# A PSUM bank for each row half of the products with v, five banks shared by both kinds of scores, and one bank for the dense products

## The chip, the core and the metric

The kernel runs on one core of a Trainium2 chip. The metric is the device time of one execution in microseconds (us). The core has a matrix engine (PE in the profile), a vector engine (DVE), a scalar engine (ACT), a general engine (POOL, GpSimd) and a queue for transfers (SP). The PE writes its results to PSUM, which has eight banks of 128 x 512 fp32 values here; DVE and ACT read them from there.

## What is computed

The kernel takes x (2048 x 512) and adds two branches that start from the same normalised rows. The reference, cut to what matters:

```
xn = layernorm(x)
q, k, v = split(xn @ wqkv)                 # 32 heads of 16
o = softmax(q @ k.T * 16 ** -0.5) @ v      # each head, 2048 x 2048 scores
out = x + o @ wo + gelu(xn @ w1 + b1) @ w2 + b2     # w1: 512 x 1792, w2: 1792 x 512
```

The results have the precision of fp32: a dense product is made of three fp16 products (high by high, high by low, low by high; `PAIRS` in the kernel).

## The kernel before

The attention is cut into 32 tiles t (8 groups of 4 heads, 4 blocks of 512 queries), and a tile into 16 units. One call of `unit` (L582) issues one unit of the first pass over the scores and, 20 units behind (`LEAD`), one unit of the second pass.

- First pass, `s_half` (L238): the scores of one head (128 queries by 512 keys) go to a bank with the tag "S", and DVE takes their maximum over the keys (L250). There are four a unit, called S0 to S3 below.
- Second pass, `e_half` (L282): the scores of one head, keys by queries and less the maximum, go to a bank with the tag "T", and ACT writes their exponential to SBUF as `pe` (L295). There are four a unit, E0 to E3.
- Products with v, `v_half` (L298): four heads by 64 rows (keys) in fp32, added up over the 16 units of a tile. There are two halves a unit. Both add to one bank (tag "V"); at the end of a tile ACT copies it to `osb` (L321).
- Dense products: everything else (the projections to q and k of later groups, called P below; the two layers of the feed-forward branch, H for the hidden one and Y for the output; the projection with wo, O) is a list of `Group`s (L408). `dense` (L565) issues three or four products of the current group in each half of a unit (`pace`: FAST, MEAN, SLOW). A P or H group has 12 products for each row half, a Y group 42.

The PE is used as eight tiles of 64 rows by 32 columns, so that an operand of 64 rows needs half of the rows, and two different streams run in the two row halves. `unit` writes the order out by hand. The first half of a unit issues S0 (rows 0 to 63), E1 (rows 64 to 127), S1 (rows 64 to 127), E0 (rows 0 to 63), then products with v in rows 64 to 127 and dense products in rows 0 to 63. The second half issues S2 (0 to 63), E3 (64 to 127), S3 (64 to 127), E2 (0 to 63), then products with v in rows 0 to 63 and dense products in rows 64 to 127. The order on every engine is the order of the program.

Since the bank of the products with v is written from the one row half and then from the other, and the bank of a dense group too, the first product of a half waits until the last products of the half before have ended: `leave` (L176) lets them count a semaphore up, and `enter` (L185) makes the next product wait for it. This is called the turn.

Banks: S has three (0 to 2), T three (3 to 5), D and V one each (L102), but a group or tile that begins takes a fresh bank from the other list and gives its own back when it ends (`hold`, L112; L303, L324, L400, L438). A bank is written again only when its reader is done: S(k+3) waits for the reduction of S(k), and the exponentials' scores for the third exponential before.

What a unit leaves for later (transfers, steps on POOL) is put in slots by `later` (L204), one slot a unit. After the first pass has ended (512 units), 20 more units run the second pass out; then `land` and the end of the program do what dense products are left.

Of the kernel before, what the change touches and what calls it, by code (L numbers as in the profile page):

```python
# [47 lines left out]
def layer_kernel(ctx: ExitStack, tc: tile.TileContext, x, wqkv, wo, w1, b1, w2, b2, out):  # L48
# [16 lines left out]
    w1_d = dram.tile([NF, P, 2, NC, P], F16, name="w1_d")  # L65
# [36 lines left out]
    free_banks = {"S": [0, 1, 2], "T": [3, 4, 5], "D": [6], "V": [7]}  # L102
# [98 lines left out]
    mt_of, ptiles, pv_of = {}, {}, {}  # L201
# [108 lines left out]

    def v_end(u):
# [12 lines left out]
        if t == NG * NQB - 1:  # L324
            later(1, lambda: last_one(osb))
            return
# [7 lines left out]

        def inverse():
            nc.vector.reciprocal(dn, dn)
            given("dve", 330)
            later(1, lambda: nc.sync.dma_start(den_d[t, 1].rearrange("h (c q) -> (h c) q", q=32), dn))
# [5 lines left out]
        def store():  # L344
# [4 lines left out]
                   (0, lambda: later(1 if n == 1 else 6, put)))  # L349
# [8 lines left out]
        n, far = (2, 3) if t < (NG - 1) * NQB else (1, 0)  # L358
        later(1, sums)
        later(2, lambda: nc.sync.dma_start(dn, den_d[t, 0].rearrange("h (c q) -> (h c) q", q=32)))  # L360
        later(2 + n + far, inverse)
        later(3 + 2 * n + far, spread)
        later(4 + 3 * n + far, store)
# [32 lines left out]
    def dbank():  # L396
        turn[0] += 1
        if pos[0] < LEAD:
            return banks("T"), None
        return hold("D", "T")  # L400

    class Group:
# [32 lines left out]
        def end(self):  # L435
            self.finish(self.bank)
            if self.key is not None:
                free_banks["T"].append(self.key)  # L438
# [35 lines left out]
    def project(m, w, sb, wh, bank, early=False):  # L474
# [6 lines left out]
        def finish(pj):  # L481
# [4 lines left out]
            stg = ph.tile([P, 2, QB], F16, name="stg", bufs=2)  # L486
# [4 lines left out]
            else:  # L491
# [5 lines left out]
                else:  # L497
                    hi = lambda: nc.gpsimd.tensor_scalar(stg[:, 0], pf, 1.0, 0.0, op0=ALU.mult, op1=ALU.add)
                    lo = lambda: nc.gpsimd.tensor_tensor(stg[:, 1], pf, stg[:, 0], op=ALU.subtract)
                    later(1, lambda: pooled((620, hi), (1160, lo), (0, lambda: later(3, put, True))), True)  # L500
# [28 lines left out]
    pos, spent, cur = [0], [False], [None]  # L529
    feed, xbs, wcs = [], {}, {}  # L530

    def fetch_x(b):
        if b < NQB:
            xbs[b] = feed[0].tile([P, 2, NC, QB], F16, name="xb", bufs=1)
            nc.sync.dma_start(xbs[b], xn_d[:, :, :, b * QB:(b + 1) * QB])

    def fetch_w1(n):
        if n < NQB * NF:
            wcs[n] = feed[0].tile([P, 2, NC, P], F16, name="wc", bufs=3)
            nc.sync.dma_start(wcs[n], w1_d[n % NF])  # L540
# [24 lines left out]
    def dense(gen, side):  # L565

        f = group(gen)
# [5 lines left out]
    def land():  # L573

        for side in range(2):
# [6 lines left out]
    def unit(gen):  # L582
# [4 lines left out]
        if u == LEAD and cur[0] is not None:  # L587
            burst(gen, cur[0].left())
        pos[0] += 1
        for a in range(2):  # L590
# [5 lines left out]
            if e >= 0:  # L596
# [33 lines left out]
    with ExitStack() as st1:  # L630
# [10 lines left out]
        def chunk(src):  # L641
            wf = ph.tile([P, 4 * W], F32, name="wch", bufs=3)
            v = wf.rearrange("p (a b) -> p a b", b=src.shape[2])
            nc.sync.dma_start(v, src)
# [14 lines left out]
        loads = []  # L659
# [13 lines left out]
        wvv = wqkv[:, 2 * D:3 * D].rearrange("(c p) n -> p c n", p=P)  # L673
        wvf = [chunk(wvv[:, :, i * W:(i + 1) * W]) for i in range(2)]
        wvh = [ph.tile([P, NC, D], F16, name="wvh", tag="wsp", bufs=2) for _ in range(2)]
# [32 lines left out]
        free = ["T", "D", "T", "V", "T", "S", "S"]  # L708
# [102 lines left out]
        free[:] = ["T", "D", "T", "V", "T"]  # L811
# [68 lines left out]
        def prepare():  # L880
# [20 lines left out]
            for n in range(16):  # L901
# [5 lines left out]
                def then(wh=None, n=n):  # L907
                    ended[0] = True
                    later(3, lambda: put(wh, n), True)

                def put(wh, n):
                    if n < 7:
                        for a in range(2):
                            for l in range(2):
                                nc.sync.dma_start(w1_d[2 * n + a][:, l], wh[:, l, :, a * P:(a + 1) * P])
                    elif n < 14:
                        nc.sync.dma_start(w2_d[:, :, 2 * n - 14:2 * n - 12, :], wh)
# [5 lines left out]
                wh = ph.tile([P, 2, 4, W] if n < 7 else [P, 2, 2, D], F16, name="wsp", bufs=2)  # L923
                k = n if n < 7 else 8
                split_steps(wh[:, 0], wh[:, 1], v, inv[:, k:k + 1], lambda wh=wh, then=then: then(wh))
# [12 lines left out]
    def mlp():  # L938
# [25 lines left out]
        for b in range(NQB):  # L964
            xb = xbs[b]
            g = m2.tile([P, 2, NF, QB], F16, name="g", bufs=1)
            for f in range(NF):
                later(1, lambda n=b * NF + f + 2: fetch_w1(n))
                wc = wcs[b * NF + f]
                if b == 0 and f >= 3:  # L970
                    nc.sync.dma_start(w2_s[:, :, f - 3:NF if f == NF - 1 else f - 2, :],
                                      w2_d[:, :, f - 3:NF if f == NF - 1 else f - 2, :])
# [156 lines left out]
```

## Time and profile before

| | |
|---|---|
| time, median of 3 runs | 1569.33 us (1568.03 to 1570.18) |
| the profiled execution | 1564.89 us |
| its span, first to last instruction | 1563.1 us |
| granted PE clock | 0.995 |
| PE, DVE, ACT, POOL busy | 97%, 91%, 88%, 42% of the span |
| reductions L250 | 2048, 683 ns each |
| exponentials L295 | 2048, 687 ns each |

All numbers of the trace come from this one execution. A row of the profile names line, engine, operation, the tiles that it writes and reads, its shape and its count; behind the bar stand the busy time, the mean of one, and the idle time before it with what ended it. PE rows hold matmuls that overlap, so their sum means little; the start times of the streams tell more. One S, E or dense stream is four matmuls side by side (count x4).

### The profile page before, as it was taken

How to read it: one execution, taken by the hardware profiler on the slowest of the kernel's cores; microseconds unless marked ns; L12 is line 12 of the kernel's file. 1: busy time of each engine (PE TensorE's matmuls, PEld its weight loads, DVE VectorE, ACT ScalarE, POOL GpSimd, SP SyncE). 2: the span in 40 equal slices, each digit the busy share in tenths (PEclk: the TensorE clock that was granted, in tenths of full speed). 3: DMA queues.
4: the chain of work that ended last, by engine and by line, in shares of the span. 5: the costliest groups of instructions: out<-in, count | busy, mean ns of one | idle time of the engine just before them, and what ended most of it. 6: DMA issues, size and time to landing. Idle time of an engine off the chain costs nothing.

```text
span 1563.1 us, 85813 instructions
## 1 busy us (share of the span) xinstructions
PE 1513.9 (97%) x38915; PEld 810.6 (52%) x38915; DVE 1424.6 (91%) x2420; ACT 1369.7 (88%) x2254; POOL 654.0 (42%) x678
## 2 busy tenths in 40 slices
PE   8998989999999999999999999999999999999988
PEld 3434545555555555555555555555555555554433
DVE  8899878899999999999999999999999999998801
ACT  4317879999999999999999999999999999998983
POOL 3113667657771113768211277741137772110000
PEclk9999999999999999999999999999999999999999
DMA  6455665532221201131111211131012201002323
GB/s 205 129 154 187 206 159 189 168 96 78 69 62 60 61 27 42 42 81 42 49 28 47 63 42 32 48 89 36 28 49 61 56 22 35 26 21 87 105 72 111
DMA packets 120246, 123.69 MB, mean 79 GB/s; under 512 B 38988, under 2 KB 90572, under 8 KB 119880
## 3 DMA queue, kind: packets, MB, share of 16 engines
q1 hardware_dynamic: 119880, 118.21, 25.8%
q8 instruction: 304, 4.98, 1.4%
q14 instruction: 62, 0.51, 0.1%
HBM read 80.61 MB, written 37.34 MB: 75 GB/s over the span
## 4 chain that ended last, share of the span: by engine, by line
PE 73%; DVE 17%; DMA 4%; issue 3%; SPq 1%; POOL 1%; ACT 1%; DVEq 0%; POOLq 0%; ACTq 0%
PE pV L169 22%; PE pD L169 17%; PE pS L169 15%; PE pT L169 15%; DVE mt L250 12%; DVE hh L979 2%; DMA m_d<-mhl 1%; PE pD L426 1%; PE pT L426 1%; DMA oc<-ot_d 1%; PE pT L519 1%; SPq L392 1%; DVE amx L648 0%; POOL osb L346 0%; PE pV L519 0%
## 5 line engine op out<-in xcount | busy, mean ns | idle before, releaser
L295 ACT ACTIVATE pe<-pT,sexp 128x512 f32<-128x512 f32 x2048 | 1268.2, 687 | 80.8 <-PE pT L169 35.0
L250 DVE TENSOR_REDUCE mt<-pS 128x1 f32<-128x512 f32 x2048 | 1288.3, 683 | 38.4 <-PE pS L169 22.8
L169 PE MATMUL pV<-pe,vv 64*32 64x512 f32 x8192 | 1082.6, 598 | 2.0 <-issue 0.9
L169 PE MATMUL pT<-qst,kst 64*32 64x512 f16 x8192 | 709.9, 379 | 14.0 <-DMA qst<-m_d 8.9
L169 PE MATMUL pS<-kst,qst 62*32 62x512 f16 x8192 | 637.7, 379 | 19.9 <-DVE mt L250 15.9
L169 PEld LDWEIGHTS <-qst 62*32 62x32 f16 x8192 | 279.5, 92 | 253.1 <-issue 115.9
L169 PEld LDWEIGHTS <-kst 64*32 64x32 f16 x8192 | 294.6, 91 | 187.7 <-issue 76.3
L169 PE MATMUL pD<-w_s,g 64*32 64x512 f16 x5376 | 365.4, 377 | 0.4 <-issue 0.4
L169 PE MATMUL pD<-xb,wc 64*32 64x512 f16 x5376 | 360.8, 377 | 0.0
L169 PEld LDWEIGHTS pV<-pe,vv 64*32 64x32 f32 x8192 | 181.9, 105 | 101.6 <-PE pS L169 7.6
L169 PEld LDWEIGHTS <-wc 64*32 64x32 f16 x5376 | 120.1, 91 | 52.7 <-issue 1.9
L997 POOL TENSOR_TENSOR xa<-xa,yt 128x512 f32<-128x512 f32 x16 | 20.5, 1278 | 283.3 <-ACT yt L995 283.3
L169 PEld LDWEIGHTS <-g 64*32 64x32 f16 x5376 | 111.5, 91 | 46.1 <-issue 2.1
L346 POOL TENSOR_TENSOR osb<-osb,rb 128x512 f32<-128x512 f32 x31 | 39.9, 1286 | 223.6 <-DMA rb<-den_d 176.2
L169 PE MATMUL pD<-xt,wqk_h 64*32 64x512 f16 x1920 | 128.6, 380 | 0.6 <-issue 0.6
L959 POOL TENSOR_TENSOR t<-hh 128x512 f32<-128x512 f32 x56 | 58.3, 1041 | 144.4 <-DVE hh L979 130.3
L961 POOL TENSOR_TENSOR t<-t,hh 128x512 f32<-128x512 f32 x56 | 71.8, 1282 | 4.7
L954 POOL TENSOR_TENSOR t<-t,hh 128x512 f32<-128x512 f32 x56 | 71.7, 1280 | 4.7
L956 POOL TENSOR_TENSOR g<-t,g 128x512 f16<-128x512 f32 x56 | 65.3, 1165 | 4.7
L169 PEld LDWEIGHTS <-wqk_h 64*32 64x32 f16 x1920 | 44.1, 92 | 20.3 <-issue 5.1
L169 PE MATMUL pD<-wo_s,oc 64*32 64x512 f16 x768 | 53.0, 392 | 0.4 <-issue 0.2
L979 DVE TENSOR_SCALAR hh<-pD,fac,b_s 128x512 f32<-128x512 f32 x56 | 45.3, 809 | 1.2
(137 smaller groups left out, 817.7 us busy)
## 6 DMA issues: line engine op xcount, KB each, us to landing
wch<-in_B_w_dram SPq DMA_DIRECT2D x28, 512.0 KB
wc<-w_d SPq DMA_DIRECT2D x56, 256.0 KB
qk_d<-stg SPq DMA_DIRECT2D x32, 256.0 KB
rb<-den_d SPq DMA_DIRECT2D x124, 64.0 KB
kst<-qk_d SPq DMA_DIRECT2D x128, 48.0 KB
qst<-qk_d SPq DMA_DIRECT2D x128, 48.0 KB
xs<-in_A_x_dram SPq DMA_DIRECT2D x16, 256.0 KB
qk_d<-stg SPq DMA_DIRECT2D x32, 128.0 KB
```

Of the source, the lines that this page charges most:

```text
L169: p = nc.tensor.matmul(*args, **kw)
L250: nc.vector.reduce_max(mt_of[t][:, n, qt, kb:kb + 1], s, axis=AX.X)
L295: nc.scalar.activation(pe, st, AF.Exp, scale=sexp[:, g // 2:g // 2 + 1])
L346: pooled((1280, lambda: nc.gpsimd.tensor_tensor(osb, osb, rb, op=ALU.mult)), (620, lambda: nc.gpsimd.tensor_scalar(ot[:, 0], osb, 1.0, 0.0 ...
L392: nc.sync.dma_start((qst, kst)[w][g % 2][p][b][64 * a:64 * a + 48, :], qk_d[w, h * DH:(h + 1) * DH, :, b * QB:(b + 1) * QB].rearrange("d j ...
L426: nc.tensor.matmul(self.bank, lhs, rhs, start=start, stop=self.last and self.over())
L954: (1280, lambda: nc.gpsimd.tensor_tensor(t1, t1, hh, op=ALU.mult)),
L956: (1160, lambda: nc.gpsimd.tensor_tensor(g[:, 1, f, :], t1, g[:, 0, f, :], op=ALU.subtract)),
L959: pooled((1040, lambda: nc.gpsimd.tensor_tensor(t1, hh, hh, op=ALU.mult)), (620, lambda: nc.gpsimd.tensor_scalar(t1, t1, 1.0, 1.0 / GELU_A ...
L961: (1280, lambda: nc.gpsimd.tensor_tensor(t1, t1, hh, op=ALU.mult)),
L979: nc.vector.tensor_scalar(hh, hp, scale, bias, op0=ALU.mult, op1=ALU.add)
L997: add = lambda: nc.gpsimd.tensor_tensor(xa, xa, yt, op=ALU.add)
```

## The change

It gives each row half of the products with v a bank of its own (6 and 7) with no turn; the first half's bank is copied by ACT half a unit earlier, and DVE adds the second one to it. From unit 20 on, S and T draw from one list of five banks (0 to 4). A dense group always has bank 5, only the dense products keep the turn, and after a group has ended `dense` leaves out one half of a unit. All H groups run at the FAST pace (before: every second one SLOW), all Y groups at MEAN (before: SLOW in the first two blocks). Transfers are cut smaller and put into slots further apart. The core of the diff:

```diff
-    w1_d = dram.tile([NF, P, 2, NC, P], F16, name="w1_d")
+    w1_d = dram.tile([NF // 2, P, 2, 2, NC, P], F16, name="w1_d")
...
-    free_banks = {"S": [0, 1, 2], "T": [3, 4, 5], "D": [6], "V": [7]}
+    free_banks = {"S": [0, 1, 2], "T": [3, 4], "D": [5], "V": [6, 7]}
...
-        if kt == 0 and a == 0:
-            pv_of[t] = hold("V", "S")
-        pv = pv_of[t][0]
+        if kt == 0:
+            pv_of[t, a] = bank_tile(6 + a, "V")
+        pv = pv_of[t, a]
...
-            product("V", pv[32 * h:32 * h + 32, :], vv[r, kt, c:c + 32], ptiles[u, h][r],
-                    start=(kt == 0 and a == 0), stop=(kt == 15 and a == 1))
+            product(None, pv[32 * h:32 * h + 32, :], vv[r, kt, c:c + 32], ptiles[u, h][r],
+                    start=kt == 0, stop=kt == 15)
+        if kt == 15 and a == 0:
+            osbs[t] = work.tile([P, QB], F32, name="osb", bufs=2)
+            nc.scalar.activation(osbs[t], pv_of.pop((t, 0)), AF.Copy)
+            given("act", 600)
...
-        pv, k = pv_of.pop(t)
-        osb = work.tile([P, QB], F32, name="osb", bufs=2)
-        nc.scalar.activation(osb, pv, AF.Copy)
-        given("act", 600)
-        free_banks["S"].append(k)
+        osb = osbs.pop(t)
+        nc.vector.tensor_tensor(osb, pv_of.pop((t, 1)), osb, op=ALU.add)
+        given("dve", 700)
...
-        n, far = (2, 3) if t < (NG - 1) * NQB else (1, 0)
-        later(1, sums)
...
+        at = (1, 3, 6, 7, 9, 12) if t < (NG - 1) * NQB else (1, 2, 5, 6, 7, 8)
+        for k, fn in zip(at, (sums, turned, inverse, keep, spread, store)):
+            later(k, fn)
...
-        if pos[0] < LEAD:
+        if pos[0] < LEAD or pos[0] >= NU + LEAD:
             return banks("T"), None
-        return hold("D", "T")
+        return hold("D", "D")
...
-            stg = ph.tile([P, 2, QB], F16, name="stg", bufs=2)
+            stg = ph.tile([P, 2, QB], F16, name="stg", bufs=3)
...
-            nc.sync.dma_start(xbs[b], xn_d[:, :, :, b * QB:(b + 1) * QB])
+            for c in range(NC):
+                later(1 + c, lambda c=c: nc.sync.dma_start(xbs[b][:, :, c], xn_d[:, :, c, b * QB:(b + 1) * QB]))
...
             done, cur[0] = cur[0], None
             done.end()
+            pause[0] = True
...
+        if pause[0]:
+            pause[0] = False
+            return
         f = group(gen)
...
-        if u == LEAD and cur[0] is not None:
-            burst(gen, cur[0].left())
+        if u == LEAD:
+            if cur[0] is not None:
+                burst(gen, cur[0].left())
+            free_banks["S"] = free_banks["T"] = free_banks["S"] + free_banks["T"]
...
-                new = r == 0 and w % 16 == 0
-                if live and not new:
+                if live:
                     v_half(w, r)
                 dense(gen, 1 - r)
-                if live and new:
-                    v_half(w, r)
-
-                for user, goes_on in (("V", live and not (r == 1 and w % 16 == 15)),
-                                      ("D", cur[0] is not None and not cur[0].over())):
-                    leave(user, goes_on)
+
+                leave("D", cur[0] is not None and not cur[0].over())
...
-                later(1 + k, lambda k=k: stacks(1, 1 - k // 4, [k % 4]), True)
-            for c in range(NC):
-                later(9 + c, lambda c=c: nc.sync.dma_start(xn_d[:, :, c, :], xt[:, :, c, :]), True)
+                later(8 + 4 * k, lambda k=k: stacks(1, 1 - k // 4, [k % 4]), True)
+            for k in range(4 * NQB):
+                c, cols = k % 4, slice(k // 4 * QB, k // 4 * QB + QB)
+                later(10 + 3 * k, lambda c=c, cols=cols: nc.sync.dma_start(xn_d[:, :, c, cols], xt[:, :, c, cols]), True)
...
-                             for c in range(NC) for i, j in PAIRS], dbank, hidden, pace=FAST if f % 2 else SLOW)
+                             for c in range(NC) for i, j in PAIRS], dbank, hidden, pace=FAST)
...
-                            lambda n, b=b: (b, n // 3) in done, pace=SLOW if b < 2 else MEAN)
+                            lambda n, b=b: (b, n // 3) in done, pace=MEAN)
...
-                if (NG - 1) * NQB + (qb if qb < NQB - 1 else -1) in ready:
+
+                if (NG - 1) * NQB + (qb if qb < NQB - 1 else -1) in ready and (pos[0] >= NU or pos[0] % 16 in range(4, 13)):
                     blocks[qb] = load_o(qb, p3), pos[0]
```

Left out are the smaller cuts of the same kind: the stores of the prepared w1 and w2 (two transfers, one a slot), the loads of w2, the later fetches of weight chunks, a third buffer for the prepared weights, and the turn of banks in the first phase, before unit 20.

More of the change, by code (lines that the diff above doesn't have):

```diff
@@ L337, in inverse, with keep @@
             given("dve", 330)
-            later(1, lambda: nc.sync.dma_start(den_d[t, 1].rearrange("h (c q) -> (h c) q", q=32), dn))
+        def keep():
+            nc.sync.dma_start(den_d[t, 1].rearrange("h (c q) -> (h c) q", q=32), dn)
         def spread():
@@ L643, in chunk @@
             v = wf.rearrange("p (a b) -> p a b", b=src.shape[2])
-            nc.sync.dma_start(v, src)
+            if len(loads) < 17:
+                nc.sync.dma_start(v, src)
+            else:
+                later(2, lambda: nc.sync.dma_start(v, src), True)
             return v
@@ L673, in layer_kernel @@
         wvv = wqkv[:, 2 * D:3 * D].rearrange("(c p) n -> p c n", p=P)
+        loads = []
         wvf = [chunk(wvv[:, :, i * W:(i + 1) * W]) for i in range(2)]
-        wvh = [ph.tile([P, NC, D], F16, name="wvh", tag="wsp", bufs=2) for _ in range(2)]
+        wvh = [ph.tile([P, NC, D], F16, name="wvh", tag="wsp", bufs=3) for _ in range(2)]
         fac_v, ready_w = [], {}
@@ L706, in stats @@
                 yield
-        free = ["T", "D", "T", "V", "T", "S", "S"]
+        free = ["T", "D", "V", "T", "V", "S", "S"]
         def vbank():
@@ L908, in then @@
                     ended[0] = True
-                    later(3, lambda: put(wh, n), True)
+                    later(2, lambda: put(wh, n), True)
                 def put(wh, n):
[L912 to L917, printed above, removed]
+                    for a in range(2):
+                        if n < 7:
+                            later(a, lambda a=a: nc.sync.dma_start(w1_d[n, :, a], wh[:, a]), True)
+                        elif n < 14:
+                            later(a, lambda a=a: nc.sync.dma_start(w2_d[:, :, 2 * n - 14 + a], wh[:, :, a]), True)
                 if n >= 14:
```

38 lines of the change are left out of this document (21 added, 17 removed).

## The prediction

> **What bounds the kernel now.** I began with the busy shares and the costliest groups of the page.
>
> ```profile
> PE 1513.9 (97%) x38915; PEld 810.6 (52%) x38915; DVE 1424.6 (91%) x2420; ACT 1369.7 (88%) x2254; POOL 654.0 (42%) x678
> L250 DVE TENSOR_REDUCE mt<-pS 128x1 f32<-128x512 f32 x2048 | 1288.3, 683 | 38.4 <-PE pS L169 22.8
> L979 DVE TENSOR_SCALAR hh<-pD,fac,b_s 128x512 f32<-128x512 f32 x56 | 45.3, 809 | 1.2
> ```
>
> PE and DVE are both near full, so shares decide nothing. I then counted the reductions L250 by stage; four of them are one unit. The columns are the stretch, its length, DVE busy with L250 (count), clock, DMA share, GB/s.
>
> ```profile
> 127.00:312.00 185.00, 152.61 (x241) 0.99 0.62 188
> 312.00:444.00 132.00, 119.39 (x193) 1.00 0.31 88
> 444.00:612.00 168.00, 161.51 (x257) 1.00 0.17 46
> 612.00:743.00 131.00, 118.68 (x192) 1.00 0.19 52
> 743.00:900.00 157.00, 149.72 (x238) 1.00 0.17 47
> 900.00:1023.00 123.00, 111.28 (x180) 1.00 0.15 41
> 1023.00:1150.00 127.00, 122.18 (x193) 1.00 0.18 50
> 1150.00:1283.00 133.00, 119.70 (x193) 1.00 0.19 50
> 1283.00:1410.00 127.00, 118.80 (x188) 1.00 0.10 26
> 1410.00:1480.00 70.00, 63.00 (x102) 0.98 0.27 83
> ```
>
> The first row is P, then H and Y alternate four times, the last is O. P: 241 / 4 = 60 units in 185 us, 3.07 us a unit. H: 758 reductions, 189.5 units in 519 us, 2.74. Y: 876, 219 units in 579 us, 2.64. O: 25.5 units in 70 us, 2.75. The rest of the span is a head of 127 us and a tail of 83.
>
> The timeline shows what makes a unit. The first two rows here are the first passes of the products with v in two successive halves near the end, where no scores are left.
>
> ```profile
> 1538.18 0.63 PE L169 MATMUL pV<-pe,vv 64*32 64x512 f32 x4 [0.23 <-PE pS L169]
> 1539.49 0.63 PE L169 MATMUL pV<-pe,vv 64*32 64x512 f32 x3 [0.23 <-PE pS L169]
> ```
>
> They are 1.31 us apart, and the PE idles 0.23 of it until the dense products before (pS here) are done: this is the turn, bare. Two halves at 1.31 are 2.62, what a Y unit takes (2.64). So in Y **the turn sets the pace**. In H, DVE adds one `hh` in 3.5 units:
>
> ```profile
> 333.54 0.81 DVE L979 TENSOR_SCALAR hh<-pD,fac,b_s 128x512 f32<-128x512 f32 x1
> 334.26 9.94 DVE L250 TENSOR_REDUCE mt<-pS 128x1 f32<-128x512 f32 x16
> 344.14 0.81 DVE L979 TENSOR_SCALAR hh<-pD,fac,b_s 128x512 f32<-128x512 f32 x1
> ```
>
> From `hh` to `hh` DVE never stops: 0.72 + 16 reductions at 0.62. There **DVE** sets the pace.
>
> **The turn goes.** The products with v no longer wait; up to 0.23 us a half, 0.46 a unit, could go. Of the 492 units with both passes, only those of Y could use it, as H is full on DVE. What is late next?
>
> **The five banks.** S and E alternate strictly, five banks rotate, five is odd: every score tile now waits for a reader on the *other* engine. Number the tiles: S0, E1, S1, E0, S2, E3, S3, E2. E3 takes the bank of S0, E2 that of S1, S2 to S3 those of exponentials. So E2, the last score before the products with v in the second half, waits until DVE has reduced S1, of the half before. In the old kernel no E waited for DVE, and S waited for the third reduction before. Behind E2 stand on the PE queue its products with v, the dense ones, and the next unit's S0. That a waiting score stops everything is in the list of waits: the PE as a whole idled for these.
>
> ```profile
> PE pS L169 <- DVE mt L250: 15.9, 47, 3.3
> PE pT L169 <- DMA qst<-m_d: 8.9, 3, 4.5
> ```
>
> This closes a ring: products with v in rows 0 to 63 (second half), then S0 in the same rows, reduction of S0, reduction of S1, E2, and in the same rows the next unit's products with v. No shift in phase shortens it. Its links are in the timeline around 558 us; there the S at 558.57 followed such products in their rows, and DVE had been idle, so it started as soon as the score was there.
>
> ```profile
> 557.70 0.62 PE L169 MATMUL pV<-pe,vv 64*32 64x512 f32 x4
> 558.57 0.42 PE L169 MATMUL pS<-kst,qst 62*32 62x512 f16 x8
> 559.10 0.40 PE L169 MATMUL pD<-w_s,g 64*32 64x512 f16 x4
> 559.32 0.61 PE L169 MATMUL pD<-w_s,g 64*32 64x512 f16 x8
> ```
> ```profile
> 559.02 0.69 DVE L250 TENSOR_REDUCE mt<-pS 128x1 f32<-128x512 f32 x1
> 559.63 0.68 DVE L250 TENSOR_REDUCE mt<-pS 128x1 f32<-128x512 f32 x1
> ```
> ```profile
> 224.40 2.83 DMA m_d<-mhl
> 227.60 1.38 DMA qst<-m_d
> 228.99 0.04 issue
> 229.03 0.58 PE pT L169 x8
> ```
>
> Products with v to S0: 0.87. S0 to its reduction: 0.45. To the next reduction: 0.61. Its duration until the bank is free: 0.68. From release to the start of a matmul: 0.04 (the last view is the chain of waits, where a PE start follows its releaser by that). One stream in front of the next in the same rows: 0.22 (dense at 559.10 and 559.32). Sum: **2.87 us a unit**, against 2.62 by the turn. The rows are those of the old kernel, the ring is new; I take it as the floor of every unit with both passes.
>
> - Y: 219 x 2.87 = 628.5 for 579: +49.5.
> - H: 189.5 x 2.87 = 543.9 for 519: +24.9.
> - O: 25.5 x 2.87 = 73.2 for 70: +3.2.
> - P: 60 x 2.87 = 172 for 185. P's 27 us over the pace of Y are 8.9 of waits for `m_d` (above) and 18 of other delays. The transfers spaced out may remove the 8.9 and the rest may hide in the longer ring (-13), or all stays (+14). I take 0.
>
> **More work on DVE.** The ring leaves DVE 2.87 - 4 x 0.61 = 0.43 idle a unit, but only in places: an operation between the two reductions of S0 and S1 and the next S0 is partly absorbed. An `hh` costs between 0 and 0.72 each. The nearest row is what it cost in the old kernel, (2.74 - 2.64) x 3.5 = 0.33: 56 x 0.33 = +18.5 (0 to 40). The new add (31 times on the path, one more in the tail) has no row; it is as large as `hh`, so 0 to 0.72, and I take 0.31: +10 (0 to 22). The small operations at a tile's end:
>
> ```profile
> L336 DVE RECIPROCAL dn<-dn 64x32 f32<-64x32 f32 x25 | 8.4, 335 | 0.0
> L272 DVE SCALAR_TENSOR_TENSOR mhl<-pS,mhl 64x64 f16<-64x64 f32 x25 | 5.4, 217 | 0.9
> L261 DVE TENSOR_REDUCE mneg<-mt 128x16 f32<-128x64 f32 x24 | 5.3, 220 | 0.8
> L271 DVE TENSOR_SCALAR mhl<-pS 64x64 f16<-64x64 f32 x25 | 5.2, 210 | 0.3
> ```
>
> They were there before, 0.98 us a tile; on the ring they count for 0 to 0.98, I take 0.5: 30 x 0.5 = +15 (0 to 30).
>
> **Pace and pause.** An H group had 3.5 units on average (FAST 3, SLOW 4) and has 3 + 0.5 now. Y: 42 products, 14 or 12 units before, 12.5 now. P: 3 before, 3.5 now. From unit 20 on: 20 P groups +10 units, Y 16 x 12.5 = 200 for 208, -8. So the dense work is as long within 2 units of some 470, and the length in units is set by the scores anyway. The single dense bank: its reader, 0.81 on DVE, has the pause of half a ring (1.4 us) and lies beside the scores; if late, the next dense product stops the PE, inside the 0 to 0.72 of `hh`.
>
> **The tail.** 22 units without S have no ring, and lose up to 0.46 each: 0 to -10, I take -5. The O groups come later (pause, loads held to certain units), so more is left for the end, where it runs as in this row, 0.22 a product:
>
> ```profile
> 1543.30 10.52 PE L426 MATMUL pD<-wo_s,oc 128*128 128x512 f16 x48
> ```
>
> Three groups of 9 more are 6 us, less what overlaps; with a possible wait for late loads 0 to +10, I take +5. Tail: 0.
>
> **At nothing.** The copy of the first bank of v is the ACT copy that was there, half a unit earlier; ACT has more room in a longer unit. More and smaller issues on SP, the third buffers, the other slots for `den_d`, POOL's steps: POOL is 42% busy and SP's waits reach the PE only through the 8.9 us; without that cover they cost at most what P's bound holds.
>
> **The sum.** 49.5 + 24.9 + 3.2 + 0 + 18.5 + 10 + 15 + 0 = +121. The span of 1563.1 becomes 1684, the profiled execution 1564.9 becomes 1686. The median of the runs is 4.4 above that execution: **1690 us**. With every open cost at its lower end (0, P -13, tail -10) it is 1569.3 + 77.6 - 23 = 1624; at its upper end (40, 22, 30, +14, +10) 1763.
>
> **The rivals.**
>
> *DVE's rate, not the ring, decides: faster.* If E2 seldom waits, because the reduction of S1 is released before its turn, a unit costs what DVE needs: 4 x 0.61 + (0.98 + 0.72) / 16 = 2.55 in Y, + 0.72 / 3.5 = 2.76 in H. Y 219 x -0.09 = -20, H +4, P -5, O -4: 1544. It decides if the ring's links sum to less than 2.55. For it: DVE is never idle in H. Against: the links are single rows of this trace and sum to 2.87. The Trainium skill (TensorEngine Tiling, "PSUM Bottleneck") says that after a 4x gain on the PE the copy out of PSUM may become the limit; read as a rate this gives the rival's 1544, and the trace agrees only in H.
>
> *The dense turn takes the place of v's: no change.* The dense products still change sides in one bank and wait. If their wait is as late as the old one, a half stays at 1.31 and the time within 1564 to 1575. For it: in the two tail rows the wait ended with the dense products. Against: nothing of the ring goes away. The Trainium skill (PSUM — Partial Sum Buffer, "PSUM bank collisions raise a hardware error") says that row tiles must not write one bank at once, so this turn has to stay; the trace shows its 0.23 only for both kinds together.
>
> *The ring with everything on it: over 1763,* if the PE and DVE delay each other in each unit.
>
> **How the numbers follow.** Ring as worked out 0.82; DVE's rate 0.09; dense turn 0.05; worse 0.04. A measurement of this kernel tells about 0.2% from no change. Faster: 0.09 + 0.01 = 0.10; same 0.02; slower 0.82 + 0.04 + 0.02 = 0.88. The range of 1610 to 1765 holds the ring's case from somewhat under its lower end; 0.18 to 0.2 is left out, most of it on the fast side.
>
> **What would show it.** Right: the waits have a new row, PE pT waiting for the reduction `mt`, of 50 us or more, or DVE idle before `mt` waiting for the PE; a Y unit takes 2.87 to 2.95 and an H unit about 3.0; DVE's share falls below 88%; in the tail the idle 0.23 before the products with v is gone. Wrong: Y units under 2.6 with DVE as full as in H (the first rival), or halves still 1.31 apart with the products with v at once and the dense ones late (the second). The likeliest error is the size of `hh` and of the tile's end on the ring.

## The result, and the profile after

The changed kernel takes **1686.72 us** (median; 1685.91 to 1688.5) against 1568.68 (1567.32 to 1570.18) for the kernel before beside it: a ratio of 1.0756, with a 95% interval of 1.0739 to 1.0773. The change costs 118 us. The forecast was 1690. The profiled execution has a span of 1684.5 us at a granted clock of 0.998.

Busy shares and the two costliest groups of the page:

```profile
PE 1647.9 (98%) x38771; PEld 869.0 (52%) x38771; DVE 1462.1 (87%) x2452; ACT 1383.2 (82%) x2254; POOL 653.0 (39%) x678
L295 ACT ACTIVATE pe<-pT,sexp 128x512 f32<-128x512 f32 x2048 | 1275.6, 687 | 179.0 <-PE pS L169 120.1
L250 DVE TENSOR_REDUCE mt<-pS 128x1 f32<-128x512 f32 x2048 | 1302.4, 684 | 127.1 <-PE pS L169 114.0
```

The page seems to say "the PE is the bound now": 98% busy. But it issued 144 matmuls fewer, and is busy 134 us longer. A stalled row half can look like that, since a stream in the other half still counts the engine as busy. What tells more is that both readers of PSUM starve. A reduction takes what it took (684 ns, 683 before), but DVE idles 127.1 us ahead of the reductions (38.4 before) and ACT 179.0 ahead of the exponentials (80.8 before), both mostly for scores of the PE.

What the PE as a whole waited for, from the list of waits (total, times, longest):

```profile
PE pT L169 <- DVE mt L250: 14.7, 37, 0.9
```

This row did not exist before: scores of the second pass wait for a reduction of the first. It is only 14.7 us, far less than the starving of the readers: the list has idle time of the whole PE, and while one row half waits the other mostly has a stream.

The reductions by stage (stretch, its length, DVE busy with L250 and count, clock, DMA share, GB/s), again P, then H and Y four times, then O:

```profile
127.00:343.00 216.00, 178.79 (x281) 1.00 0.51 161
343.00:495.00 152.00, 125.28 (x198) 1.00 0.24 73
495.00:641.00 146.00, 127.81 (x201) 1.00 0.16 47
641.00:791.00 150.00, 124.21 (x196) 1.00 0.17 51
791.00:937.00 146.00, 127.79 (x201) 1.00 0.14 41
937.00:1088.00 151.00, 123.93 (x196) 1.00 0.13 38
1088.00:1233.00 145.00, 126.98 (x200) 1.00 0.16 45
1233.00:1384.00 151.00, 124.62 (x197) 1.00 0.16 45
1384.00:1530.00 146.00, 127.36 (x201) 1.00 0.09 23
1530.00:1606.00 76.00, 64.20 (x103) 1.00 0.19 58
```

Four reductions are a unit. Y: 803 / 4 = 200.75 units in 583 us, **2.90** (2.64 before). H: 787 / 4 = 196.75 in 604 us, **3.07** (2.74). P: 70.25 in 216 us, 3.07 (3.07). O: 25.75 in 76 us, 2.95 (2.75). The ring, followed through one Y unit; first PE rows of the timeline (start, duration), then those of DVE:

```profile
559.73 0.61 PE L169 MATMUL pV<-pe,vv 64*32 64x512 f32 x4
560.58 0.40 PE L169 MATMUL pS<-kst,qst 62*32 62x512 f16 x4
562.37 0.40 PE L169 MATMUL pT<-qst,kst 64*32 64x512 f16 x4
562.59 0.61 PE L169 MATMUL pV<-pe,vv 64*32 64x512 f32 x4
```
```profile
554.63 0.22 DVE L261 TENSOR_REDUCE mneg<-mt 128x16 f32<-128x64 f32 x1
...
561.03 0.69 DVE L250 TENSOR_REDUCE mt<-pS 128x1 f32<-128x512 f32 x1 [0.38 <-PE pS L169]
561.64 0.68 DVE L250 TENSOR_REDUCE mt<-pS 128x1 f32<-128x512 f32 x1
...
563.90 0.69 DVE L250 TENSOR_REDUCE mt<-pS 128x1 f32<-128x512 f32 x1 [0.28 <-PE pS L169]
```

Which reduction is which follows from `mneg`, which comes right behind S3 of a tile's last unit: counted on from there in fours, the one at 561.03 is that of S0. Products with v at 559.73; S0 at 560.58 (+0.85); its reduction at 561.03 (+0.45), after DVE had idled 0.38; that of S1 at 561.64 (+0.61), done at 562.32 (+0.68); the waiting E2 at 562.37 (+0.05), though its rows were free from 562.10 on, 0.22 after S2; products with v again at 562.59 (+0.22). That is 2.86 us round. The next unit's first reduction begins at 563.90, 2.87 after this one, and DVE idles 0.28 to 0.38 in each unit.

The first half of a unit closes a second ring of the same length, with dense products in the place of those with v: S2 at 561.88, its reduction at 562.33, that of S3 at 562.94, done at 563.62, and E0 of the next unit, which takes the bank of S3, at 563.68, 0.06 later; the dense products behind E0 follow 0.22 after it in the same rows, and the next S2 behind them.

In the tail, where no first-pass scores are left, the wait of the turn is gone from the rows:

```profile
1647.51 0.61 PE L169 MATMUL pV<-pe,vv 64*32 64x512 f32 x4
1648.75 0.61 PE L169 MATMUL pV<-pe,vv 64*32 64x512 f32 x4
...
1654.16 0.61 PE L169 MATMUL pV<-pe,vv 64*32 64x512 f32 x4
1655.27 0.61 PE L169 MATMUL pV<-pe,vv 64*32 64x512 f32 x4
```

The last two are 1.11 us apart, where it was 1.31 with an idle 0.23. Not every half is so short: the first two are 1.24 apart, and the five halves from 1644.05 to 1649.87 take 1.16 us on average, against 1.28 for the 17 halves from 1517.71 to 1539.49 in the kernel before. So the turn is cheaper, as the change meant it to be, and far more is lost elsewhere.

### The profile page after: what moved, and what is told of

The parts are those of the page before. It is cut to its first block, busy times and chain, and to the rows that moved or that the text cites. A ratio compares the mean times of both kernels' runs of the same rounds, so it can differ in the third digit from the quotient of the medians.

```text
span 1684.5 us, 85602 instructions
## 1 busy us (share of the span) xinstructions
PE 1647.9 (98%) x38771; PEld 869.0 (52%) x38771; DVE 1462.1 (87%) x2452; ACT 1383.2 (82%) x2254; POOL 653.0 (39%) x678
## 4 chain that ended last, share of the span: by engine, by line
PE 87%; DVE 7%; issue 1%; ACT 1%; SPq 1%; DMA 1%; POOL 0%; DVEq 0%; ACTq 0%; POOLq 0%
PE pV L169 24%; PE pT L169 22%; PE pS L169 19%; PE pD L169 18%; DVE mt L250 4%; DVE hh L996 1%; PE pT L431 1%; DVE amx L660 1%; PE pT L524 1%; SPq L397 1%; PE pS L431 1%; ACT pe L295 0%; PE pD L431 0%; PE pV L431 0%; PE pS L268 0%
## 5 line engine op out<-in xcount | busy, mean ns | idle before, releaser
L295 ACT ACTIVATE pe<-pT,sexp 128x512 f32<-128x512 f32 x2048 | 1275.6, 687 | 179.0 <-PE pS L169 120.1
L250 DVE TENSOR_REDUCE mt<-pS 128x1 f32<-128x512 f32 x2048 | 1302.4, 684 | 127.1 <-PE pS L169 114.0
L169 PE MATMUL pV<-pe,vv 64*32 64x512 f32 x8192 | 1097.0, 592 | 0.4 <-issue 0.3
L169 PE MATMUL pT<-qst,kst 64*32 64x512 f16 x8192 | 817.5, 380 | 15.3 <-DVE mt L250 14.7
L169 PEld LDWEIGHTS <-kst 64*32 64x32 f16 x8192 | 340.5, 90 | 359.6 <-issue 321.0
L169 PEld LDWEIGHTS <-qst 62*32 62x32 f16 x8192 | 288.9, 91 | 224.8 <-issue 121.7
L169 PE MATMUL pD<-xb,wc 64*32 64x512 f16 x5376 | 351.5, 377 | 0.0
L169 PEld LDWEIGHTS pV<-pe,vv 64*32 64x32 f32 x8192 | 245.2, 105 | 35.0 <-issue 1.2
L169 PEld LDWEIGHTS <-wc 64*32 64x32 f16 x5376 | 135.0, 92 | 45.9
L169 PEld LDWEIGHTS <-g 64*32 64x32 f16 x5376 | 135.6, 91 | 35.4
L970 POOL TENSOR_SCALAR t<-t,gs 128x512 f32<-128x512 f32 x56 | 38.8, 692 | 28.1 <-ACT t L965 28.1
```

The costliest lines, as they stand in the source:

```text
L169: p = nc.tensor.matmul(*args, **kw)
L250: nc.vector.reduce_max(mt_of[t][:, n, qt, kb:kb + 1], s, axis=AX.X)
L295: nc.scalar.activation(pe, st, AF.Exp, scale=sexp[:, g // 2:g // 2 + 1])
L970: pooled((690, lambda: nc.gpsimd.tensor_scalar(t1, t1, 1.0, gs[:, 1:2], op0=ALU.add, op1=ALU.mult)), (1280, lambda: nc.gpsimd.tensor_tenso ...
```

## The experiments

The theory was: E2 waits for DVE's reduction of S1, since S and E alternate over five banks, and this closes a ring of 2.87 us. Its rivals were other parts of the change: the dense products in one bank with a turn, the new work on DVE, the paces. Times are ratios to the kernel before, run beside them, with a 95% interval. Units are counted as above, over one Y stage and the H stage after it (which is why the kernels before and after stand at 2.61 and 2.92 for Y below, and at 2.64 and 2.90 over all four stages).

**1. Five banks alone.** The kernel before, with S and T drawing on five banks from unit 20; turn, dense banks that change, paces and transfers as before. A spare bank X takes the place of the one that dense groups and tiles borrowed.

```diff
-    free_banks = {"S": [0, 1, 2], "T": [3, 4, 5], "D": [6], "V": [7]}
+    free_banks = {"S": [0, 1, 2], "T": [3, 4], "D": [5], "V": [6], "X": [7]}
...
+            free_banks["S"] = free_banks["T"] = free_banks["S"] + free_banks["T"]
```

> The kernel before with one part of the change alone: from unit 20 on S and T draw from one list of five banks; the products with v keep their one bank (with a spare one for the change of tiles, as for the dense groups) and their turn; no pause, no add, old paces and transfers. Theory (ring): a unit of 2.87 us and more again, the time 1650 to 1700 us. Rival (the sharing costs little, the rest of the change does it): 1570 to 1600 us.

Measured: 1699.65 us, 1.0844 [1.0798, 1.0889]. Its waits, and its Y and H stage:

```profile
PE pT L169 <- DVE mt L250: 21.3, 56, 3.1
```
```profile
471.00:645.00 174.00, 152.87 (x240) 1.00 0.14 41
645.00:785.00 140.00, 114.17 (x180) 1.00 0.18 50
```

Y 174 / 60 = 2.90, H 140 / 45 = 3.11, and the new row of waits: **the shared five banks alone make the whole slowdown.** The rest of the change, added to it, gives some 14 us back (1.0844 to 1.0756).

**2. The other order.** The changed kernel with E issued ahead of S in each pair, so that the reduction of S1 is no longer what E2 waits for.

```diff
-                if u < NU:
-                    s_half(u, b)
                 if 0 <= e < NU:
                     e_half(e, b ^ 1)
+                if u < NU:
+                    s_half(u, b)
```

> The changed kernel with one thing else: in each pair the second-pass score is issued before the first-pass score (E1, S0, E0, S1 in place of S0, E1, S1, E0). Same five shared banks, same work, same rows. Now E2 takes the bank of S0 instead of S1, and E1 of the next unit that of S1, two halves later. Theory (the ring of score, reduction, bank, products with v): the ring loses the second reduction, 0.87 + 0.45 + 0.68 + 0.04 + 0.22 = 2.26 us, and a unit falls to what the rows or DVE need: Y 2.55 to 2.60, H 2.74 to 2.80 us a unit, the time 1545 to 1575 us. Rival (the new add on DVE, the pause, the single dense bank or the longer DVE queue cost the time): nothing of that is touched, Y stays near 2.9 us and the time at 1670 to 1690 us.

Measured: 1652.24 us, 1.0544 [1.0508, 1.058], Y 2.87, H 2.93. **The expectation failed.** Worked through bank by bank, the order is now E1, S0, E0, S1, E3, S2, E2, S3, and with five banks S3 takes the one of E0: the last score of a half waits for the second exponential of the half before. I had taken a wait off DVE and put the same wait on ACT. Its rows show it, PE and then ACT:

```profile
559.80 0.61 PE L169 MATMUL pV<-pe,vv 64*32 64x512 f32 x4
560.66 0.40 PE L169 MATMUL pT<-qst,kst 64*32 64x512 f16 x4
562.43 0.40 PE L169 MATMUL pS<-kst,qst 62*32 62x512 f16 x4
562.64 0.61 PE L169 MATMUL pV<-pe,vv 64*32 64x512 f32 x4
```
```profile
561.11 0.69 ACT L295 ACTIVATE pe<-pT,sexp 128x512 f32<-128x512 f32 x1 [0.21 <-PE pT L169]
561.70 0.68 ACT L295 ACTIVATE pe<-pT,sexp 128x512 f32<-128x512 f32 x1
```

This is the half in which S1 is last and takes the bank of E2. Products with v at 559.80; E3, in the same rows, at 560.66 (+0.86); its exponential at 561.11 (+0.45); that of E2 at 561.70 (+0.59), done at 562.38 (+0.68); S1 at 562.43 (+0.05), though its rows were free from 562.03 on, 0.22 after E1; products with v at 562.64 (+0.21). Sum 2.84, the unit measured 2.87.

**3. No sharing.** The changed kernel with three banks for S and two for T, each list its own.

```diff
-            free_banks["S"] = free_banks["T"] = free_banks["S"] + free_banks["T"]
```

> The changed kernel without the joining of the two lists: S keeps three banks, T has two, the other banks as changed. Theory (ring): no second-pass score waits for DVE any more, so a Y unit falls from 2.9 to 2.55 to 2.70 us (two banks for T may make it wait for ACT a little), the time 1550 to 1610 us. Rival (too few banks for the scores, whichever way they are shared; or add and pause): 1660 us and more.

Measured: 1708.79 us, 1.0902 [1.086, 1.0944], Y 161 / 53.75 = 3.00, H 2.99: slower than with sharing, and the expectation failed again. Its timeline shows why, PE and ACT:

```profile
545.58 0.61 PE L169 MATMUL pV<-pe,vv 64*32 64x512 f32 x4
546.28 0.39 PE L169 MATMUL pT<-qst,kst 64*32 64x512 f16 x4
546.44 0.61 PE L169 MATMUL pS<-kst,qst 62*32 62x512 f16 x8
...
548.33 0.40 PE L169 MATMUL pT<-qst,kst 64*32 64x512 f16 x4
...
548.55 0.61 PE L169 MATMUL pV<-pe,vv 64*32 64x512 f32 x4
```
```profile
547.02 0.69 ACT L295 ACTIVATE pe<-pT,sexp 128x512 f32<-128x512 f32 x1 [0.46 <-PE pS L169]
547.60 0.68 ACT L295 ACTIVATE pe<-pT,sexp 128x512 f32<-128x512 f32 x1
```

Products with v at 545.58; S0 at 546.44 (+0.86); the first exponential at 547.02 (+0.58), after ACT had idled 0.46; the second at 547.60 (+0.58), done at 548.28; E2 at 548.33 (+0.73); products with v at 548.55 (+0.22). Sum 2.97, the unit measured 3.00. With two banks for T, E2 waits for E0. One step of this sum is argued, not shown: the first exponential is that of E1, which started at 546.28, and I count it from S0 (see the last section). **The theory became wider:** with five banks a score at the end of a half waits for the second reader of the half before, on DVE or on ACT, whether the banks are shared or dealt; with three banks for each kind it waits for the first, one reader earlier.

**4. The dealt five, the other way round.** From unit 20 two banks for S, three for T. Now S2 and S3 wait for the reductions of S0 and S1.

```diff
-            free_banks["S"] = free_banks["T"] = free_banks["S"] + free_banks["T"]
+            free_banks["T"].append(free_banks["S"].pop(0))
```

> The changed kernel with two lists in place of one shared one, from unit 20 on two banks for S and three for T (e2_split had three and two). Wider theory: S3, the last first-pass score of a half, then waits for the second reduction of the half before, with the products with v behind it on the queue: Y units 2.85 to 2.95 us, the time 1665 to 1705 us, so no way to deal out five banks helps. Rival (it was ACT's readers that made e2_split slow, and T with three banks is free of them): Y 2.6 to 2.7 us, the time 1560 to 1600 us.

Measured: 1704.15 us, 1.0894 [1.0866, 1.0921], Y 2.94, H 3.12. As the wider theory has it; the PE as a whole waits 41.2 us for reductions before first-pass scores (15.9 in the kernel before).

**5 to 7. A shorter reduction, in three kernels.** The edit is the same in each: a maximum takes only half of its keys.

```diff
-        nc.vector.reduce_max(mt_of[t][:, n, qt, kb:kb + 1], s, axis=AX.X)
+        nc.vector.reduce_max(mt_of[t][:, n, qt, kb:kb + 1], s[:, :QB // 2], axis=AX.X)
```

In the changed kernel:

> The changed kernel, but each reduction takes the maximum over 256 of the 512 keys of a score tile (the other half is left out of the maximum). Banks, order and turn as changed. Theory (ring of score, two reductions, bank, products with v): both reductions in the ring get shorter by about 0.27 us each, the ring falls to about 2.33 us and the rows decide instead: a Y unit 2.50 to 2.62 us, an H unit 2.60 to 2.72 us, the time 1500 to 1560 us. Rival (not the reductions: the turn of the dense products, the exponentials or the number of score banks hold a unit at 2.87): Y stays at 2.80 us or more, the time over 1640 us.

In the kernel before, as its reference:

> The kernel before with the same half of the maxima left out. Theory (the turn sets the pace of Y there, DVE that of H): a Y unit stays at 2.60 to 2.64 us though DVE has a third less to do, an H unit falls from 2.74 to 2.62 to 2.66 us, the time 1540 to 1558 us. Rival (DVE sets the pace everywhere): Y falls to 2.5 us or less, the time under 1525 us. Against e5_halfmax it also tells what the lost turn is worth where no ring stands.

And in the kernel of experiment 2, where the ring should go over ACT:

> e1_swap (second-pass score first in each pair) with half of the keys left out of each maximum, as in e5_halfmax. After e1_swap and e2_split the theory is wider: with five banks the last score of a half waits for the second reader of the half before, and the swap only moves that reader from DVE to ACT. Then a cheaper reduction gains nothing here: Y units stay at 2.78 to 2.90 us, the time at 1600 to 1650 us, though the same edit without the swap gave 1541 us. Rival (DVE still holds the swapped order): Y falls to 2.65 us or less, the time to 1530 to 1570 us.

Measured: 1540.99 us, 0.9829 [0.9808, 0.985]; 1542.16, 0.9837 [0.9816, 0.9858]; 1645.76, 1.052 [1.0492, 1.0548]. The Y stages, in that order:

```profile
461.00:602.00 141.00, 81.22 (x214) 1.00 0.18 50
```
```profile
445.00:600.00 155.00, 90.61 (x240) 1.00 0.16 46
```
```profile
490.00:644.00 154.00, 83.99 (x214) 1.00 0.16 46
```

A reduction takes 0.42 us on average in all three (0.68 before), and 0.38 to 0.39 of DVE's busy time in these stages, where one overlaps the next. Y falls from 2.92 to 141 / 53.5 = 2.64 in the changed kernel, and the whole slowdown goes. It hardly moves in the kernel before (2.61 to 155 / 60 = 2.58, DVE 58% busy with reductions in it): there DVE does not hold the pace, as the theory of the turn has it, and the gain is H's (2.76 to 2.67). And it does not move at all with E first (2.88 against 2.87), with DVE as empty: that ring does not go over DVE. So DVE's reductions are the link of the first ring and not of the second; that ACT's exponentials are the link of the second is read from the rows of experiment 2 and was not tried by a cheaper exponential. What sets the 2.64 and the 2.77 that are left in the first of them (Y was expected at 2.50 to 2.62, H at 2.60 to 2.72) was not told apart. In the second, Y was expected at 2.60 or more and H at 2.66 or less: 0.02 and 0.01 off.

**8. Half of the units mirrored.** In the second half of each unit S3, E2, S2, E3, so that the score that waits stands in the rows of the dense products and not in those of the products with v.

```diff
+                c = b ^ a
                 if u < NU:
-                    s_half(u, b)
+                    s_half(u, c)
                 if 0 <= e < NU:
-                    e_half(e, b ^ 1)
+                    e_half(e, c ^ 1)
```

> The changed kernel with the second half of a unit mirrored: S3, E2, S2, E3 in place of S2, E3, S3, E2. The last score, which waits for the second reduction of the half before, is then not in the rows of the products with v, so these need not wait for its stream. Theory (ring): one link, the stream of 0.22 us, falls to about 0.02 us, a Y unit goes from 2.87 to 2.65 to 2.72 us, the time to 1590 to 1625 us. Rival (the wait for the bank is there, but what sets the pace is the queue of exponentials, which keeps its order of two a half): Y stays at 2.80 us or more, the time at 1650 us or more.

Measured: 1644.94 us, 1.0492 [1.047, 1.0515], Y 2.80, H 3.00: by the time between the theory and its rival, by Y at the rival's edge. The waits:

```profile
PE pT L169 <- DVE mt L250: 8.4, 23, 1.2
```

The waits of E fall from 14.7 to 8.4 us, but do not go. Behind the waiting E there now stand three or four dense streams in its rows, and then the scores and the products with v of the next half. The ring of the first half, over E0, was left out of the expectation and has its waiting score where it was. Which ring sets the 2.80 is not settled: the one that I can follow through single rows sums to about 2.5.

**9. The turn put back.** Experiment 2 with its products with v again in a turn, though they write two banks: what is the turn worth where a ring stands?

```diff
-            product(None, pv[32 * h:32 * h + 32, :], vv[r, kt, c:c + 32], ptiles[u, h][r],
+            product("V", pv[32 * h:32 * h + 32, :], vv[r, kt, c:c + 32], ptiles[u, h][r],
...
-                leave("D", cur[0] is not None and not cur[0].over())
+                for user, goes_on in (("V", live and w % 16 < 15),
+                                      ("D", cur[0] is not None and not cur[0].over())):
+                    leave(user, goes_on)
```

> As e1_swap, but the products with v take part in the turn again as before the change (except at the last unit of a tile), though they keep a bank for each row half. Theory: the turn sets 1.31 us a half again, Y units of 2.62 to 2.66 us, the time 10 to 25 us over that of e1_swap. Rival (the turn never cost anything that the scores or DVE would not have taken anyway): within 4 us of e1_swap.

Measured: 1660.54 us, 1.0596 [1.0568, 1.0623], 8.3 us over experiment 2; Y 2.90 and H 2.95 (2.87 and 2.93). Nearly half of the 8 us is in the tail (82 us from the last reduction's end, against 78), where there is no ring. That is less than the 10 to 25 expected and more than the rival's 4, and Y is far from the 2.62 to 2.66 expected: under a ring the turn is worth little, some 5 us here.

**10. Two turns.** The kernel before, whose products with v and dense products waited for one shared semaphore, with a semaphore for each: every kind now waits for its own kind alone. Banks and all else as before.

```diff
-    turns = tc.alloc_semaphore("turns")
+    turns = {k: tc.alloc_semaphore(f"turns{k}") for k in "VD"}
...
-        if goal[0] is not None:
-            p._wait_ge(turns, counted[0])
+        if goal[user] is not None:
+            p._wait_ge(turns[user], counted[user])
```

> The kernel before, with one edit: the products with v and the dense products each have a turn of their own, so the first product with v waits only for the last one with v, and the first dense product only for the last dense one. Banks as before. Theory (the turn sets the pace of Y; the dense products are issued behind those with v, and their end is told later): part of the 0.23 us idle a half goes, a Y unit falls from 2.64 to 2.52 to 2.60 us, H stays within 0.03 us (DVE), the time 1545 to 1563 us. Rival (the wait for the products with v alone is as long): within 3 us of the kernel before.

Measured: 1546.64 us, 0.9861 [0.984, 0.9883], **faster than the kernel before, by 1.4%.** Its tail, and its Y and H stage:

```profile
1521.05 0.63 PE L169 MATMUL pV<-pe,vv 64*32 64x512 f32 x4
1522.20 0.63 PE L169 MATMUL pV<-pe,vv 64*32 64x512 f32 x4
```
```profile
450.00:604.00 154.00, 146.96 (x240) 1.00 0.16 46
604.00:726.00 122.00, 110.35 (x180) 1.00 0.20 58
```

1.15 us for this half (1.17 on average over the 19 halves from 1499.94 to 1522.20; 1.28 before, 1.16 in the changed kernel), Y 154 / 60 = 2.57 for 2.61, H 2.71 for 2.76. So the turn did cost time, and in the tail, where no reduction stands in the way, nearly all that the change gains there is to be had with no bank moved: the long part of the wait was for the *other* kind. H was expected to stay within 0.03 and fell by 0.05: the turn had a part in H's pace too.

**11. Two turns and the spaced transfers.** Experiment 10 with the transfer edits of the change, but for the held loads for O.

```diff
-                later(1 + k, lambda k=k: stacks(1, 1 - k // 4, [k % 4]), True)
+                later(8 + 4 * k, lambda k=k: stacks(1, 1 - k // 4, [k % 4]), True)
```

> e8_two_turns (the kernel before with separate turns) plus the change's transfers: smaller ones, further apart, with the third buffers; none of its banks, pause or paces. What the spaced transfers are worth where no ring hides it: the projections took 3.07 us a unit before, 27 us over the pace of Y, 8.9 us of it waits of the PE for m_d. Theory: 3 to 12 us off e8_two_turns, 1535 to 1544 us. Rival (the waits for m_d come from their own chain of five transfers, not from what stands in front of them): within 3 us of e8_two_turns.

Measured: 1545.4 us, 0.9883 [0.9864, 0.9903]: no gain over experiment 10 that can be told. The trace has both a gain and a loss. P is faster (258 reductions in its 185 us, 237 in experiment 10). But a new wait stands in the list, and SP's queue shows it:

```profile
PE pT L169 <- DMA qst<-m_d: 9.1, 1, 9.1
```
```profile
1449.56 2.60 SPq L1023 DMA_DIRECT2D oc<-ot_d  x4
...
1457.41 2.35 SPq L1028 DMA_DIRECT2D ac<-acc_d  x4
1460.22 1.92 SPq L276 DMA_DIRECT2D m_d<-mhl  x2
```

Sixteen transfers for O keep SP's queue from 1449.56 to 1459.76, and `m_d`, on which the last tile's scores wait, comes behind them at 1460.22, though DVE had its source `mhl` ready at 1452.17. This is what the change holds the O loads for.

**12. And the held loads.**

```diff
-                if (NG - 1) * NQB + (qb if qb < NQB - 1 else -1) in ready:
+                if (NG - 1) * NQB + (qb if qb < NQB - 1 else -1) in ready and (pos[0] >= NU or pos[0] % 16 in range(4, 13)):
```

> e9_turns_spaced plus the last transfer edit of the change: the loads for the product with wo are held to units 4 to 12 of a tile while the first pass runs. In e9_turns_spaced sixteen transfers of 256 KB went out at 1449 to 1460 us, straight ahead of the transfers for m_d at 1460, and the PE waited 9.1 us for them in the last tile. Theory: that wait falls under 3 us, the time to 1535 to 1542 us. Rival (the loads then come later and the dense products with wo are left for the end, so the tail grows by what the wait gave): 1543 to 1550 us.

Measured: **1534.14 us, 0.9785 [0.9765, 0.9805]**, 2.15% under the kernel before and the best of all. The wait for `m_d` is gone from the list; dense products wait once for `oc` instead, 3.2 us. Its P and Y:

```profile
127.00:307.00 180.00, 155.61 (x245) 1.00 0.60 190
435.00:588.00 153.00, 147.11 (x242) 1.00 0.17 50
```

P is at 180 / 61.25 = 2.94 a unit (3.07 before), Y at 153 / 60.5 = 2.53, H at 2.72. DVE is busy 96% of this Y stage with reductions alone. The share proves nothing, it was 97% in the kernel before (151.88 of 157 us, 241 reductions); but a reduction has 0.61 of busy time here, as when each follows the last at once, and had 0.63 there. With the 0.98 of a tile's end, 4 x 0.61 + 0.98 / 16 = 2.50 is an estimate of what DVE needs. That its rate is the bound of Y now is likely, and not shown.

All in one table (us a unit, the stages quoted or counted alike):

| kernel | Y | H | ratio to before |
|---|---|---|---|
| before | 2.61 | 2.76 | 1 |
| after | 2.92 | 3.08 | 1.0756 |
| 1 five banks alone | 2.90 | 3.11 | 1.0844 |
| 2 E first | 2.87 | 2.93 | 1.0544 |
| 3 three and two | 3.00 | 2.99 | 1.0902 |
| 4 two and three | 2.94 | 3.12 | 1.0894 |
| 5 after, half the maxima | 2.64 | 2.77 | 0.9829 |
| 6 before, half the maxima | 2.58 | 2.67 | 0.9837 |
| 7 E first, half the maxima | 2.88 | 2.92 | 1.052 |
| 8 mirrored | 2.80 | 3.00 | 1.0492 |
| 9 E first and turn | 2.90 | 2.95 | 1.0596 |
| 10 two turns | 2.57 | 2.71 | 0.9861 |
| 11 two turns, transfers | 2.52 | 2.73 | 0.9883 |
| 12 and held loads | 2.53 | 2.72 | 0.9785 |

## Why the prediction was right, and where it was not

**The turn was the bound of Y: right.** Experiments 6 and 10 show it from both sides: an emptier DVE gains 0.02 a unit there, a shorter turn 0.04. **That only Y could use a shorter turn, H being full on DVE: wrong.** In experiment 10 H gains 0.05.

**The ring and its floor of 2.87: right.** The links came out one by one in the quoted unit: 0.85, 0.45, 0.61, 0.68, 0.05 and 0.22, for 0.87, 0.45, 0.61, 0.68, 0.04 and 0.22. Two stretches of eight Y units of the changed kernel, the first with a tile's `dn` and `mneg` alone, the second with `mhl` and the new add:

```profile
532.00:554.94 22.94, 20.35 (x33) 1.00 0.43 128
554.94:578.50 23.56, 20.39 (x33) 1.00 0.16 44
```

22.94 / 8 = 2.87. What the argument lacked was its generality: it saw the ring over E2 and not the one over E0, and put the fault on the odd count and on DVE, while experiments 2 to 4 show that five banks close a ring over either reader in every order tried.

**`hh` at 0.33 on the ring: too small.** A Y and the H stage after it, of the changed kernel:

```profile
495.00:651.00 156.00, 136.41 (x214) 1.00 0.16 46
651.00:791.00 140.00, 115.62 (x182) 1.00 0.18 52
```

156 / 53.5 = 2.916 and 140 / 45.5 = 3.077. They differ by 0.16 a unit, at 3.5 units to one `hh` 0.56 each: 31 us and not 18.5, within the bounds given. **A tile's end with the new add at 0.81: too large.** The two stretches differ by 0.62, for 0.81; over the 26 tiles of H, Y and O that is 16 us (25 was set for all 30). The two together were set at 43.5; over their 423.25 units these stages took 1263 us, 48 more than 2.87 a unit.

**P at nothing: right.** From unit 20 on, P took 185 us for 60 units before and runs at 216 / 70.25 = 3.07 now: the pace stayed, the groups take the ten units more that the pause gives them. That spacing the transfers helps (P at 2.94 in experiment 12) does not show here; that the ring hides it is argued.

**The tail at nothing: 5 us off.** From the last reduction's end to the end of the span it was 84 us and is 79, as the loss of the turn alone would give. Up to the last reduction the kernel is 126 us later, for +121 in the sum. The two errors cancel: the span was forecast at 1684 and came to 1684.5, and that closeness is luck, the floor of 2.87 is not.

**What would show it: one sign was wrong.** The new row of waits has 14.7 us, and 50 or more was asked for, or DVE idle for the PE, which came. The list has idle time of the whole PE; a ring that stops one row half at a time leaves little of it. The other signs came: DVE idle ahead of `mt` (127.1, of which 114.0 for scores of the PE), its share at 87%, Y at 2.90, H at 3.07, no idle 0.23 in the tail.

**The rivals.** DVE's rate (1544) is out: DVE idles 127.1 us, and Y is at 2.90 for its 2.55. The dense turn in place of v's (a time as before) is out by the time, and by halves of 1.16 in the tail. The ring with everything on it (over 1763) is out: the ring hides part of what DVE adds.

The Trainium skill (Perfetto Trace Analysis, "Optimizing Tensor Performance") advises to rotate independent matmul groups through different PSUM banks so that the reading of one overlaps the next; the change follows that, and experiment 1 shows that rotating is not enough: five banks over two readers take 2.90 us a unit, six in two lists 2.61.

Not tried one by one: the pause, the paces, the single dense bank and the new add. Experiment 1 bounds them with the turn and the transfers, together at about -14 us where the ring stands.

## What to carry to other kernels

When buffers are shared out anew, write down for each write which reader of which earlier tile it waits for, and follow the program order behind it until it comes round to that reader: a ring's latencies sum to a floor that no engine's busy share shows, and taking a buffer from one reader can put the same wait on another. Before paying for a wait with a buffer, look whom it waits for: here a semaphore for each kind of product gave 1.4% with no bank moved, and with the transfers spaced and held 2.15%. A list of idle times of an engine that runs two streams says little; ask its readers how long they starve.

## What the runs showed of the hardware

**Streams start out of the order of issue, and their ends seem to be told in it.** In the kernel of experiment 3, E1 started at 546.28 and the S0 issued ahead of it, in the other row half, at 546.44. ACT, idle, began the exponential of E1 only at 547.02: 0.74 us after E1's start, 0.58 after S0's. In the quoted Y unit of the changed kernel E1 started at 560.21, S0 at 560.58, and the exponential of E1 at 561.15: 0.94 after its own start, 0.57 after S0's, ACT idle again. In experiment 2, where E is issued first, the exponential began 0.45 after the start of E3; the reduction of S2, which is issued behind E3 and started ahead of it at 560.37, began at 561.17, 0.80 after its own start. That ends are told in order is argued from these rows, not shown by an experiment. The Trainium skill (TensorE: Matmul & The Clock Gate, "The mechanism") says that matmuls keep program order in start and end; the starts here differ from it by 0.16 and 0.37 us, the ends would agree.

**A wait of one product for another on the same engine** costs little when it is for the same kind a half earlier (1.17 us a half on average in the tail of experiment 10, 1.16 with no turn for v) and some 0.11 more when it is for both kinds (1.28).

**One queue's issue order decides waits far away:** sixteen transfers, 0.6 us each on SP's queue (10.2 us in all), held `m_d` back for 8 us and the PE waited 9.1; with them held back by some units that wait was gone.
